# Two float32 filler products of 256 columns between the landings of the last expert's left columns

## The chip, the cores and the metric

The kernel runs on one core of one Trainium2 chip. The metric is the device time of one execution in microseconds; lower is better. TensorE (PE) multiplies, VectorE (DVE) and ScalarE (ACT) evict from PSUM and do elementwise work, GpSimd (POOL) issues the loads that change the type, and SyncE (SP) issues the stores.

## The reference: pooled attention, then a mixture of experts by slots

```python
# q, k, v: (8, 8, 576, 64); k and v are means over 8 positions: 72 keys
scores = scale * q @ k_p.T;  attn = softmax(scores);  x = attn @ v_p
# x as (4608, 512); phi: (512, 32); w1: (8, 512, 1024); w2: (8, 1024, 512)
logits = x @ phi
d = softmax(logits, over tokens);  slot_input = d.T @ x     # 32 slots, 4 per expert
for e in range(8):
    slot_out[e] = relu(slot_input[e] @ w1[e]) @ w2[e]
c = softmax(logits, over slots);  out = c @ slot_out        # (4608, 512)
```

Inputs and output are float32; the kernel computes in bfloat16 with float32 sums.

## The kernel before

**The first part** goes over four pairs of batches. For each it pools keys and values, turns the queries, computes scores and attention, and collects the slots' inputs. The exponentials of all tokens' logits, transposed, stay in the tile cT. POOL's queue issues all weight loads, which change float32 to bfloat16 on the way: w1 to its own tile, w2 of experts 0 to 3 into `big`, of 4 and 5 into `qTa`, of expert 6 into `xsa` in two loads (chunks 0 to 4, chunks 5 to 7; lines 482 and 483). w2 of the last expert, 7, comes in six loads of its own (line 499): first the left 256 columns in the three PIECES of chunks 0 to 2, 3 to 6 and 7, then the right 256 columns in the same three.

**The second part** starts at line 511. There the order of PE, ACT, DVE and SP is that of the text: each engine runs its instructions in the order in which they are written, and waits where a semaphore makes it wait. `hidden` and `turn_hidden` compute the first layer for all experts. `second_layer(e, j0, j1, half)` adds chunks j0 to j1 of expert e to `so_ps`, one product a chunk; with `half` only the left or right 256 columns. Four chunks in a row go to four strips of 32 columns of the array, and so run beside each other.

`busy(n)` (line 583) multiplies a 128 by 128 float32 view of cT with n columns of the same view, into the scratch tile `idle`, which nothing reads. The kernel before calls it five times, with 512 columns each time: around the row sums (lines 665 to 668), after expert 5 (line 671) and in the middle of expert 6 (line 673).

**The place of the change** is lines 674 to 677: the second half of expert 6, then chunks 0 to 2 of the last expert's left columns, which wait for the first landing, then chunks 3 to 6, which wait for the second, then `begin(0)`. In `begin` ScalarE scales the sum so far into `so_a` (line 625). TensorE multiplies the carried part of chunk 7 (`from_z`, line 630) and `so_a` (line 633) for the first four tiles of the output; then it adds chunk 7 to `so_ps`, and ScalarE makes the final `so` (line 648). `tiles` and the loop at line 685 make the other tiles: one product each (line 611), an eviction by ACT (line 588) or DVE (line 590) that divides by the row sum, and stores by SP (line 607): eight of 256 KB for the first eight tiles, in halves, then 1, 1, 2 and 3 MB.

Of the kernel before, what the change touches and what calls it, by code (L numbers as in the profile page):

```python
# [18 lines left out]
def kernel(  # L19
# [525 lines left out]
    def second_layer(e, j0=0, j1=FJ, half=None):  # L545
        cols = slice(0, DM) if half is None else halves[half]
        for fj in range(j0, j1):
            g = fj % NG
            nc.tensor.matmul(out=so_ps[g * NS:(g + 1) * NS, cols], lhsT=hT[:, e, fj],
                             rhs=w2_at[e, fj] if half is None else w2_half[fj, half],  # L550
                             start=(e == 0 and fj < NG), stop=(e == E - 1 and fj >= NG), skip_group_check=True)
# [31 lines left out]
    def busy(n):  # L583
        nc.tensor.matmul(out=idle[:, 0:n], lhsT=cTf[:, 0:128], rhs=cTf[:, 0:n], start=True, stop=True)
# [37 lines left out]
    def begin(half):  # L622

        cols = halves[half]
        scaled(0, so_a[:, cols], so_ps[:, cols], recC)
        f = [ps_f.tile([128, DM], FP, name="f_ps", tag="f")[:, 0:HC] for _ in range(CARRY)]

        def from_z(n, j0, j1):
            for j in range(j0, j1):
                nc.tensor.matmul(out=f[n], lhsT=zT[:, j - J7, n], rhs=w2_half[j, half], start=(j == J7), stop=False)  # L630

        def from_slots(n):
            nc.tensor.matmul(out=f[n], lhsT=tokens(n), rhs=so_a[:, cols], start=False, stop=True)  # L633

        for n in range(2):
            from_z(n, J7, FJ - 1)
        for n in range(2):
            from_z(n, FJ - 1, FJ)
        for n in range(2):
            from_slots(n)  # L640
        put(0, cols, 0, f[0])
        put(1, cols, 1, f[1])
        store(0, 0, 2, cols)
        second_layer(E - 1, J7, FJ, half)
        for n in range(2, CARRY):
            from_z(n, J7, FJ)
            from_slots(n)
        scaled(0, so[:, cols], so_ps[:, cols], recC)
        put(2, cols, 1, f[2])
        put(3, cols, 0, f[3])  # L650
        store(0, 2, 4, cols)
# [20 lines left out]
    second_layer(E - 2, 0, 5)  # L672
    busy(512)
    second_layer(E - 2, 5, FJ)
    second_layer(E - 1, 0, 3, 0)
    second_layer(E - 1, 3, J7, 0)
    begin(0)
    tiles(4, 6, 0)
# [41 lines left out]
```

## Time and profile before

| | us |
|---|---|
| median of 3 runs | 175.56 (175.49 to 175.78) |
| the profiled execution's own time | 175.54 |
| its span, first to last instruction | 173.8 |
| PE busy | 128.0 (74%) |
| DVE busy | 93.0 (54%) |
| ACT busy | 89.1 (51%) |
| POOL busy | 21.7 (12%) |

The profile is of one execution. The span runs from the first to the last instruction; the time of the execution has what lies around it as well. The page cuts the span into 40 slices of 4.3 us and gives the busy share of each engine in tenths. Other views list groups of instructions by line, the chain of work that ended last, the instructions in order of time, and the busy time, granted TensorE clock and DMA share in stretches that one can choose. In a row of the timeline stand the start, the busy time, the engine, the line and the tiles, and in brackets the idle time before it with what ended it. Matmuls are pipelined and their ends are modelled; a few records can be missing. A DMA share above 1 means that transfers overlapped on an engine.

### The profile page before, as it was taken

How to read it: one execution, taken by the hardware profiler on the slowest of the kernel's cores; microseconds unless marked ns; L12 is line 12 of the kernel's file. 1: busy time of each engine (PE TensorE's matmuls, PEld its weight loads, DVE VectorE, ACT ScalarE, POOL GpSimd, SP SyncE). 2: the span in 40 equal slices, each digit the busy share in tenths (PEclk: the TensorE clock that was granted, in tenths of full speed). 3: DMA queues.
4: the chain of work that ended last, by engine and by line, in shares of the span. 5: the costliest groups of instructions: out<-in, count | busy, mean ns of one | idle time of the engine just before them, and what ended most of it. 6: DMA issues, size and time to landing. Idle time of an engine off the chain costs nothing.

```text
span 173.8 us, 2847 instructions
## 1 busy us (share of the span) xinstructions
PE 128.0 (74%) x1104; PEld 69.0 (40%) x1104; DVE 93.0 (54%) x255; ACT 89.1 (51%) x171; POOL 21.7 (12%) x37
## 2 busy tenths in 40 slices
PE   0005787999899999999699999637999995897000
PEld 0002443665555665556444665422453322432000
DVE  5403344397868589786972856750542002799000
ACT  3201249885887739888490895463021103898000
POOL 7000111022100040009000104001410000000000
PEclk9999999999999999999957999955799999999555
DMA  5999999999999999999999999999999999999994
GB/s 192 247 216 223 216 216 212 220 214 212 218 218 214 215 219 214 218 215 214 215 219 211 223 211 219 213 221 211 223 211 219 208 197 177 301 390 447 404 453 183
DMA packets 8989, 41.13 MB, mean 237 GB/s; under 512 B 640, under 2 KB 4736, under 8 KB 5136
## 3 DMA queue, kind: packets, MB, share of 16 engines
q0 software_dynamic: 6080, 30.48, 85.5%
q1 hardware_dynamic: 2896, 10.49, 15.3%
q8 instruction: 8, 0.13, 0.3%
q14 instruction: 5, 0.04, 0.1%
HBM read 61.93 MB, written 9.44 MB: 411 GB/s over the span
## 4 chain that ended last, share of the span: by engine, by line
PE 40%; DMA 20%; ACT 16%; DVE 11%; issue 4%; POOL 1%; DVEq 0%; ACTq 0%; POOLq 0%
DMA xsa<-in_moe_w_dram 14%; PE pool_ps L227 9%; ACT exa L301 7%; DMA phi_f<-in_moe_phi_dram 7%; PE u_ps L314 6%; PE sc L299 6%; PE G_ps L349 4%; PE q_ps L259 4%; DVE w_sb L590 4%; DVE xsa L325 4%; PE lg_ps L342 2%; PE turn_ps L243 2%; ACT vmeans L233 2%; DVE rec L319 2%; PE f_ps L611 2%
## 5 line engine op out<-in xcount | busy, mean ns | idle before, releaser
L301 ACT ACTIVATE exa<-sc 72x576 bf16<-72x576 f32 x64 | 39.3, 653 | 6.6 <-PE u_ps L314 3.4
L325 DVE TENSOR_TENSOR xsa<-u_ps,rec 128x384 bf16<-128x384 f32 x66 | 35.8, 553 | 1.2
L314 PE MATMUL u_ps<-vp,exa 72*128 72x97 bf16 (+1 forms) x304 | 25.0, 215 | 4.6 <-DVE xsa L325 3.6
L314 PEld LDWEIGHTS <-exa 72*128 72x128 bf16 (+1 forms) x320 | 17.7, 103 | 15.6 <-DVE xsa L325 6.1
L299 PE MATMUL sc<-qTa,kp 64*72 64x288 bf16 x128 | 22.0, 313 | 1.6 <-ACT exa L301 1.0
L227 PE MATMUL pool_ps<-big,pmat 128*128 128x512 bf16 x64 | 17.5, 398 | 0.7 <-ACT qTa L263 0.6
L319 DVE RECIPROCAL rec<-u_ps 128x4 f32<-128x4 f32 x69 | 11.2, 174 | 11.5 <-PE u_ps L314 11.2
L179 PE MATMUL phi_ps<-spread,sel 128*128 128x256 bf16 x4 | 1.3, 394 | 15.1 <-DVE spread L174 15.1
L349 PE MATMUL G_ps<-xsa,ee 128*128 128x512 bf16 x36 | 11.5, 481 | 1.2 <-ACT ee L343 1.2
L259 PE MATMUL q_ps<-ident,big 128*128 128x128 bf16 x144 | 11.6, 219 | 0.8 <-DVE qTa L265 0.2
L299 PEld LDWEIGHTS <-kp 64*72 64x72 bf16 x128 | 7.9, 109 | 8.4 <-issue 3.0
L235 DVE TENSOR_REDUCE rsum<-rest_ps 128x64 f32<-128x512 f32 x8 | 5.5, 692 | 9.6 <-PE rest_ps L231 9.6
L265 DVE COPY qTa<-q_ps 128x768 bf16<-128x768 bf16 x16 | 8.7, 552 | 3.1 <-PE q_ps L259 3.0
L611 PE MATMUL f_ps<-so,cT 128*128 128x512 bf16 (+1 forms) x36 | 9.6, 353 | 0.7 <-ACT w_sb L588 0.6
L259 PEld LDWEIGHTS <-big 128*128 128x128 bf16 x144 | 8.6, 97 | 3.3 <-issue 1.8
L590 DVE TENSOR_SCALAR w_sb<-f_ps,recR 128x512 f32<-128x512 f32 x14 | 9.3, 741 | 0.1
L263 ACT COPY qTa<-q_ps 128x768 bf16<-128x768 bf16 x8 | 6.4, 795 | 5.7 <-PE q_ps L259 5.7
L590 DVE TENSOR_SCALAR exa<-f_ps,recR 128x256 f32<-128x256 f32 x8 | 3.8, 483 | 9.9 <-PE f_ps L633 9.6
L233 ACT CAST vmeans<-pool_ps 128x1024 bf16<-128x1024 f32 x4 | 4.0, 1012 | 9.2 <-PE pool_ps L227 9.2
L227 PEld LDWEIGHTS <-pmat 128*128 128x128 bf16 x64 | 5.9, 101 | 6.8 <-issue 2.1
L588 ACT ACTIVATE w_sb<-f_ps,recR 128x512 f32<-128x512 f32 x14 | 8.4, 696 | 0.2
L499 POOL DMA_DIRECT2D xsa<-in_moe_w_dram x6 | 4.1, 695 | 27.4 <-PE G_ps L349 13.2
(109 smaller groups left out, 160.9 us busy)
## 6 DMA issues: line engine op xcount, KB each, us to landing
w_sb<-in_moe_w_dram POOLq DMA_DIRECT2D x2, 3072.0 KB, 38.3
big<-in_q_dram POOLq DMA_DIRECT2D x4, 1152.0 KB, 12.8
big<-in_v_dram POOLq DMA_DIRECT2D x4, 1152.0 KB, 16.7
big<-in_moe_w_dram POOLq DMA_DIRECT2D x1, 4096.0 KB, 32.3
big<-in_k_dram POOLq DMA_DIRECT2D x3, 1152.0 KB, 21.4
out_dram<-w_sb SPq DMA_DIRECT2D x1, 3072.0 KB, 10.9
w_sb<-in_moe_w_dram POOLq DMA_DIRECT2D x2, 1024.0 KB, 19.6
qTa<-in_moe_w_dram POOLq DMA_DIRECT2D x1, 2048.0 KB, 33.2
```

The lines of the kernel that those rows point to most:

```text
L227: nc.tensor.matmul(out=ps, lhsT=pmat, rhs=src[:, t:full * POOL:POOL, :], start=(t == 0), stop=(t == POOL - 1))
L259: nc.tensor.transpose(out=ps[:, t].rearrange("p n i -> p (n i)"), in_=q_sb[pair][:, tt:tt + 2, :].rearrange("p t d -> p (t d)"), identity= ...
L265: nc.vector.tensor_copy(out=dst, in_=ps)
L299: nc.tensor.matmul(out=ps[:, r, 0:S // 2], lhsT=kp[pair][rows, n], rhs=qT[pair][rows, n].rearrange("p t i -> p (t i)"), start=True, stop=True)
L301: nc.scalar.activation(out=dst.rearrange("p r (i t) -> p r i t", t=NU), in_=ps[:, :, 0:S // 2].rearrange("p r (t i) -> p r i t", i=NI), fu ...
L314: nc.tensor.matmul(out=ps[rows, hh], lhsT=ex[b][:, hh].rearrange("p r t -> p (r t)")[:, c:c + rows.stop - rows.start], rhs=vp[(2 * pair + ...
L319: nc.vector.reciprocal(out=rec, in_=ps[:, :, XW])
L325: nc.vector.tensor_tensor(out=dst, in0=ps[:, :, 0:XW], in1=rec.rearrange("p h -> p h ()").to_broadcast([128, HQ, XW]), op=ALU.mult)
L349: nc.tensor.matmul(out=ps, lhsT=ee[:, t].rearrange("p g s -> p (g s)"), rhs=x[:, t, :, 0:D], start=(t == 0), stop=(t == 8))
L588: nc.scalar.activation(out=dst, in_=src, func=AF.Copy, scale=by)
L590: nc.vector.tensor_scalar(out=dst, in0=src, scalar1=by, scalar2=None, op0=ALU.mult)
L611: nc.tensor.matmul(out=ps, lhsT=tokens(n), rhs=so[:, cols], start=True, stop=True)
```

## The change

Two calls of `busy(256)` are added to the written order: one between the last chunks of expert 6 and chunks 0 to 2 of the last expert's left columns, one between these and chunks 3 to 6.

```diff
     second_layer(E - 2, 0, 5)
     busy(512)
     second_layer(E - 2, 5, FJ)
+    busy(256)
     second_layer(E - 1, 0, 3, 0)
+    busy(256)
     second_layer(E - 1, 3, J7, 0)
     begin(0)
     tiles(4, 6, 0)
```

The function that is called is unchanged:

```python
    def busy(n):
        nc.tensor.matmul(out=idle[:, 0:n], lhsT=cTf[:, 0:128], rhs=cTf[:, 0:n], start=True, stop=True)
```

## The prediction

> **What bounds the kernel now.** I read the page's slices first, for what is busy at the end, then the chain of work that ended last, then the TensorE timeline around the place of the change, then the stores.
>
> ```profile
> DMA  5999999999999999999999999999999999999994
> ```
>
> The DMA engines are busy from the second slice to the last but one. TensorE is not: the change sits in a stretch in which it waits for weights.
>
> The chain of work that ended last (start, us, step) passes that stretch:
>
> ```profile
> 121.63 23.80 DMA xsa<-in_moe_w_dram
> 145.47 0.32 PE so_ps L549 x4
> 145.81 0.48 ACT so_a L588
> 146.33 0.28 PE f_ps L633
> 146.64 0.34 ACT exa L588
> 147.01 0.48 ACT so L588
> 147.53 0.38 PE f_ps L611 x2
> 148.13 0.34 PE f_ps L611 x2
> 148.49 0.47 ACT exa L588
> 148.97 0.37 ACT so_a L588
> 149.38 0.28 PE f_ps L633
> 149.69 0.47 ACT exa L588
> ```
>
> For 23.8 us the chain is one transfer, the second piece of the last expert's left columns. From 145.47 it is a relay of TensorE and ScalarE steps. So what counts is whether the four products at 145.47 start when their weights land, and how fast the relay behind them runs. The TensorE rows of the timeline (start, busy us, operation, then idle time before it and what ended it):
>
> ```profile
> 142.04 1.12 PE L584 MATMUL idle_ps<-cT 128*128 128x512 f32 x2
> 143.18 0.40 PE L549 MATMUL so_ps<-xsa,hT 128*32 128x512 bf16 x3
> 144.18 0.29 PE L549 MATMUL so_ps<-xsa,hT 128*32 128x256 bf16 x3 [0.60 <-DMA xsa<-in_moe_w_dram]
> 145.47 0.29 PE L549 MATMUL so_ps<-xsa,hT 128*32 128x256 bf16 x4 [1.00 <-DMA xsa<-in_moe_w_dram]
> 145.81 0.38 PE L630 MATMUL f_ps<-xsa,zT 128*128 128x256 bf16 x2
> ```
>
> Each call of busy(512) is two float32 passes in the trace. The three products of expert 6's last chunks end at 143.58. TensorE then waits 0.60 us for the first left piece, runs three products, waits 1.00 us for the second, runs four, and goes on. The two fillers go into these two waits.
>
> Behind the relay stand the stores, by the DMA issues of the SP queue (first and last start, us):
>
> ```profile
> L607 SPq DMA_DIRECT2D out_dram<-exa x8: 372/422/455, 147.3 to 152.1; - x8
> L607 SPq DMA_DIRECT2D out_dram<-w_sb x4: 332/338/345, 153.3 to 161.2; - x4
> out_dram<-w_sb SPq DMA_DIRECT2D x1, 3072.0 KB, 10.9
> ```
>
> The last store leaves at 161.2 and takes 10.9 us to land. I take it that a shift of the relay shifts the end by as much. That is an upper bound for either sign, since a store that stands in a queue hides part of a shift.
>
> **The change, part by part.** Nothing is removed or moved. Two calls of busy(256) are added, each one float32 product of a cT block with 256 columns of cT into the scratch tile idle_ps, which no one reads. By the x2 of the row above that is two weight loads and two matmuls a call, so four of each in all. There are no new DMAs, no new waits on another engine (cT was written long before) and nothing for SP, POOL, ScalarE or VectorE. What can be late is what stands behind a filler on TensorE: the three products on the first piece, the four on the second, and through them ScalarE's so_a.
>
> The trace has no float32 product of 256 columns. These rows bound it:
>
> ```profile
> L584 PE MATMUL idle_ps<-cT x10: 590/592/697, 136.2 to 142.6; 128*128 128x512 f32 x10
> L611 PE MATMUL f_ps<-so,cT 128*128 128x512 bf16 x28 | 8.3, 377 | 0.6 <-ACT w_sb L588 0.6
> ...
> L611 PE MATMUL f_ps<-so,cT 128*128 128x256 bf16 x8 | 1.4, 272 | 0.1
> 143.09 0.19 PEld L549 LDWEIGHTS <-hT 128*32 128x32 bf16 x4 [0.76 <-issue]
> 141.73 0.38 PE L549 MATMUL so_ps<-xsa,hT 128*32 128x512 bf16 x1
> ```
>
> Step by step:
>
> - From 512 to 256 columns a bf16 product falls by 377 - 272 = 105 ns. A float32 pass of 512 columns takes 592 ns, that is 215 ns above bf16, so it streams like 1024 bf16 columns and its half saves 2 x 105 = 210 ns.
> - busy(512) holds the engine from 142.04 to 143.09, where the next product's weight load starts: 1.05 us. For 256 columns I estimate 1.05 - 2 x 0.21 = 0.63 us. The ends of the range are nothing (all of it beside other work) and the 1.05 us of the wide form (no saving at all). I take 0.63, because the bf16 pair shows that time goes with columns.
> - The last product ahead of a filler started at 141.73 and the filler at 142.04: 0.31 us. So the first new filler starts at 143.18 + 0.31 = 143.49 and is through at 144.12. With the 0.09 us from the weight load at 143.09 to the product at 143.18, the products on the first piece could start at 144.21. They start at 144.18 now: 0.03 us late, and nobody waits for them before the second piece.
> - The second filler starts at 144.21 + 0.31 = 144.52, is through at 145.15, and the four products could start at 145.24. Their weights let them start at 145.47. So 0.23 us are left, and both fillers are covered by the landings. Price: nothing.
> - If that cover were gone, the price would be what sticks out. With 1.05 us each, the first is through at 144.54 (products at 144.63), the second runs 144.94 to 145.99, and the four products start at 146.08: 0.61 us late.
>
> Below nothing the added work could come out only through TensorE's clock in the relay. By windows (stretch, length, PE busy, ..., granted clock, DMA share, GB/s):
>
> ```profile
> 82.98:86.39 3.41, 2.15 (x28) 1.17 (x26) 3.19 (x10) 0.88 (x3) 0.00 (x0) 1.00 1.04 219
> 86.39:89.81 3.42, 3.36 (x23) 1.61 (x24) 2.74 (x9) 3.17 (x6) 0.00 (x0) 0.50 1.03 216
> 110.29:113.70 3.41, 1.95 (x24) 1.28 (x24) 2.41 (x10) 1.29 (x6) 0.00 (x0) 1.00 1.03 216
> 113.70:117.11 3.41, 0.99 (x8) 0.64 (x8) 2.10 (x7) 2.37 (x11) 0.00 (x0) 0.50 1.03 216
> 141.01:144.42 3.41, 2.80 (x15) 0.70 (x14) 0.00 (x0) 0.00 (x0) 0.00 (x0) 1.00 1.31 192
> 144.42:147.83 3.41, 2.15 (x18) 1.08 (x14) 0.97 (x2) 1.64 (x4) 0.00 (x0) 1.00 1.23 166
> 147.83:151.25 3.42, 2.98 (x24) 1.61 (x24) 2.30 (x5) 2.97 (x8) 0.00 (x0) 1.00 0.91 301
> 143.20:146.60 3.40, 1.61 (x14) 0.67 (x13) 0.00 (x0) 0.47 (x1) 0.00 (x0) 1.00 1.45 195
> ```
>
> The clock is 1.00 throughout 141.01 to 151.25, so in this execution there is nothing for a filler to win. But it fell to 0.50 at 86.39 and at 113.70, after 3.41 us with TensorE busy 2.15 and 1.95 us. These two times lie 27.31 us apart, eight times 3.41, and so do the edges that I chose here. The stretch 144.42 to 147.83, with the same 2.15 us, kept its clock. A stretch of the same length that began at 143.20 has only 1.61 us. Had the edges lain there, the clock would by these rows have been halved in the middle of the relay.
>
> The Trainium skill speaks against a win here: "TensorE: Matmul & The Clock Gate", section on HAM oscillation, gives as its rule no idle gaps above about 3.4 us. With a longest gap of 1.00 us here the clock is never at stake by that rule, and the fillers are worth nothing. The trace doesn't bear the rule out as a bound: ahead of 86.39 the longest idle time in the timeline is well under a microsecond.
>
> ```profile
> 85.09 0.36 PE L314 MATMUL u_ps<-vp,exa 72*128 72x97 bf16 x4 [0.50 <-DVE xsa L325]
> ```
>
> The same page (Part 1) says that the window of about 3.4 us runs freely and isn't tied to the kernel's start; the distance of eight times 3.41 agrees, and one trace can't show where the edges lie in other executions.
>
> Sum: nothing on the path. The profiled execution took 175.54 us, 1.74 more than its span of 173.8, and the median of the runs shown is 175.56, 0.02 above it. **Forecast: 175.5 us, no change.** A measurement of this kernel can tell about 0.2%, or 0.35 us, from no change.
>
> **The rivals.**
>
> *The clock (faster).* If the edges of those 3.41 us stretches lie differently in most executions, the clock is half from about 146.6 to 150.0 before the change, and the fillers prevent it: they bring that stretch from 1.61 us to 1.61 + 2 x 0.63 = 2.87 us busy. The price of half clock, from the same nine products at full and at half clock:
>
> ```profile
> 105.23 2.10 PE G_ps L349 x9
> 119.61 4.02 PE L349 MATMUL G_ps<-xsa,ee 128*128 128x512 bf16 x9 [1.22 <-ACT ee L343]
> ```
>
> That is (4.02 - 2.10) / 9 = 0.21 us for 512 columns, and 0.11 for 256. The relay has two, two and one such products between 147.53 and 149.66: five, 0.5 us. So this rival gives 175.56 - 0.5 = 175.05 us; with a product more or less on the path, 174.9 to 175.2. For it: the trace halves the clock after stretches busier than the one at 143.20. Against it: the execution that kept its clock took 175.54, and the three runs spread only from 175.49 to 175.78. Were most of them slowed by half a microsecond, the profiled one should lie 0.5 us below them, and it doesn't.
>
> *The filler is too long (slower).* If a float32 pass of 256 columns costs as much as one of 512, the four products start 0.61 us late, as worked out above, and the relay and the stores with them: 176.15 us. It decides from the point at which both fillers together take more than 2 x 0.63 + 0.23 = 1.5 us. Landings closer together than now would do the same. For it: 0.23 us isn't much, and the width of the float32 form is not in the trace. Against it: the bf16 rows go with columns.
>
> *No effect at all, because nothing runs in the gap.* Were the fillers' result thrown away by the compiler, the time would be the same 175.5; the existing fillers, also never read, appear in the trace, so I give it no chance of its own.
>
> **How the numbers follow.** Hidden fillers, unchanged clock: 0.58, with its own range 175.3 to 175.8 from the spread of the three runs and 0.2 us of luck below. The clock: 0.28. The filler too long: 0.14. These are also the chances of within 0.2%, faster and slower. The range goes from 175.0 to 176.0: it takes in most of the clock's 174.9 to 175.2 and the half of the slower case in which the fillers stick out by less than 0.45 us.
>
> **What would show it.** Right: four more passes of L584 (x14 instead of x10) with some 380 ns each, the idle times of 0.60 and 1.00 us almost gone, the four products still starting within 0.1 us of 145.47 with a DMA as their releaser, the relay as it was. The clock rival: the relay from 146.6 to 150 shorter than now in the changed kernel, or a kernel before that shows 0.50 there in another execution. The slower rival: the four products released by no DMA, and later than 145.6. The forecast is wrong if the landings themselves move, or if a shift of the relay of some tenths, in either direction, shows in the time.

## The result, and the profile after

The changed kernel is slower: a median of 176.81 us (175.55 to 177.88, 22 runs) against 175.92 us (175.49 to 177.25, 22 runs) for the kernel before, measured side by side. The ratio is 1.0037 with a 95% interval of 1.0019 to 1.0055. The forecast was 175.5 us and no change. In the tables and ranges below, three executions far outside all others (230.06, 209.3 and 198.64 us) and one slow run of the changed kernel (178.66 us, over 1.5% above its fastest) are left out.

The lowest runs of the two kernels are the same, 175.55 and 175.49 us. The profiled execution of the changed kernel took 176.39 us (span 174.6), 0.85 more than that of before. Its fillers are what was forecast. The group of the scratch tile in the profile after:

```profile
L584 PE MATMUL idle_ps<-cT x14: 379/593/697, 137.6 to 146.0; 128*128 128x512 f32 x10, 128*128 128x256 f32 x4
```

Four passes more, 379 ns where the prediction had some 380. The surprise is in the TensorE timeline of the profile after (start, busy us, operation, idle time before it):

```profile
126.61 3.64 PE L528 MATMUL h_ps<-w_sb,siT 128*32 128x512 bf16 x64
...
144.50 0.40 PE L549 MATMUL so_ps<-xsa,hT 128*32 128x512 bf16 x3
144.82 0.70 PE L584 MATMUL idle_ps<-cT 128*128 128x256 f32 x2
145.45 0.29 PE L549 MATMUL so_ps<-xsa,hT 128*32 128x256 bf16 x3
145.67 0.70 PE L584 MATMUL idle_ps<-cT 128*128 128x256 f32 x2
146.30 0.29 PE L549 MATMUL so_ps<-xsa,hT 128*32 128x256 bf16 x4
146.52 0.39 PE L630 MATMUL f_ps<-xsa,zT 128*128 128x256 bf16 x2
```

A filler holds TensorE from 144.82 to 145.45, 0.63 us as estimated. But no bracket with a DMA is left: TensorE waits for no landing. It reaches expert 6's last products at 144.50, not 143.18, so the weights of the first piece already lie there, and both fillers stand in its way. The chain of waits says the same. Where the chain of before had 23.8 us of one transfer, that of after runs through TensorE:

```profile
143.51 1.06 PE idle_ps L584 x2
144.57 0.33 PE so_ps L549 x3
144.89 0.63 PE idle_ps L584 x2
145.74 0.63 PE idle_ps L584 x2
146.37 0.25 PE so_ps L549 x4
```

The trace's record of the second piece's landing is 145.43 us before and 145.68 after. The four products start at 145.47 and at 146.30. So of the 0.83 us, 0.25 are the landing, and 0.58 are the fillers, which stick out behind it. The later landing isn't their doing: expert 6's first chunks landed at 141.55 instead of 141.23, also late, over 3 us ahead of the first filler. The same second landing was at 145.72 in `e7` below, which has no filler there, and at 145.46 in `e15`, the changed kernel again. The relay that follows isn't slower: the end comes 29.73 us after the first product of `from_z` before (175.54 - 145.81) and 29.87 us after (176.39 - 146.52).

TensorE is late from further up. The first layer started at 125.21 in the profile before; here are that row, and then two rows of the profile after:

```profile
125.21 3.64 PE L528 MATMUL h_ps<-w_sb,siT 128*32 128x512 bf16 x64
```

```profile
105.92 2.12 PE L349 MATMUL G_ps<-xsa,ee 128*128 128x512 bf16 x9
...
121.06 3.98 PE L349 MATMUL G_ps<-xsa,ee 128*128 128x512 bf16 x9 [1.22 <-ACT ee L343]
```

Against 105.23 and 119.61 in the rows of before, that is 0.69 us late at the third pair's gather and 1.45 at the last. Of the 0.69 us, 0.54 were there at the start of the kernel: the first product of line 231 starts at 18.80 us before and at 19.34 after, and the seven of line 227 ahead of it take 2.50 us before and 2.87 after. That looks like half clock, but isn't shown: the windows read 1.00 there in both. For the 0.76 us that came in between the two gathers the clock gives the reason. By windows, after:

```profile
107.79:111.20 3.41, 2.84 (x48) 2.09 (x45) 2.82 (x9) 1.37 (x4) 0.58 (x2) 1.00 1.03 216
111.20:114.62 3.42, 2.71 (x23) 1.87 (x20) 1.96 (x7) 1.28 (x6) 0.00 (x0) 0.50 1.05 220
114.62:118.03 3.41, 1.20 (x11) 0.65 (x8) 1.78 (x7) 1.84 (x9) 0.00 (x0) 0.50 1.02 214
118.03:121.44 3.41, 1.52 (x5) 0.56 (x6) 0.57 (x2) 2.15 (x5) 0.00 (x0) 0.50 1.03 216
121.44:124.86 3.42, 3.42 (x9) 1.22 (x8) 0.00 (x0) 0.00 (x0) 2.53 (x4) 0.50 1.06 223
```

Four stretches of 3.41 us at half clock, from 111.20, where the profile before had three, from 113.70. Between the products that start at 111.04 and at 114.31 in the profile before, which mostly run while only the execution after is at half clock, its lateness grows from 0.75 to 1.44 us. The fillers of the change, which run 20 us behind these stretches, can't have caused this, and `e15` below, the same kernel, has three such stretches, from 114.05. It is how that execution fell.

### The profile page after: what moved, and what is told of

It reads as the page before. It is cut to its first block, busy times and chain, and to the rows that moved or that the text cites. A ratio compares the mean times of both kernels' runs of the same rounds, so it can differ in the third digit from the quotient of the medians.

```text
span 174.6 us, 2855 instructions
## 1 busy us (share of the span) xinstructions
PE 130.3 (75%) x1108; PEld 70.2 (40%) x1108; DVE 92.9 (53%) x255; ACT 89.0 (51%) x171; POOL 21.7 (12%) x37
## 4 chain that ended last, share of the span: by engine, by line
PE 54%; ACT 15%; DVE 12%; DMA 7%; issue 4%; POOL 1%; DVEq 0%; ACTq 0%; POOLq 0%
PE pool_ps L227 9%; ACT exa L301 7%; PE u_ps L314 7%; DMA phi_f<-in_moe_phi_dram 7%; PE G_ps L349 6%; PE sc L299 6%; PE q_ps L259 4%; DVE w_sb L590 4%; PE idle_ps L584 4%; DVE xsa L325 3%; PE so_ps L549 3%; PE lg_ps L342 2%; PE R_ps L418 2%; PE h_ps L528 2%; PE turn_ps L243 2%
## 5 line engine op out<-in xcount | busy, mean ns | idle before, releaser
L314 PE MATMUL u_ps<-vp,exa 72*128 72x97 bf16 (+1 forms) x304 | 25.7, 218 | 4.1 <-DVE xsa L325 3.9
L314 PEld LDWEIGHTS <-exa 72*128 72x128 bf16 (+1 forms) x320 | 18.2, 104 | 15.4 <-DVE xsa L325 6.5
## 6 DMA issues: line engine op xcount, KB each, us to landing
big<-in_q_dram POOLq DMA_DIRECT2D x4, 1152.0 KB, 12.8
```

What stands on the lines that cost most here:

```text
L314: nc.tensor.matmul(out=ps[rows, hh], lhsT=ex[b][:, hh].rearrange("p r t -> p (r t)")[:, c:c + rows.stop - rows.start], rhs=vp[(2 * pair + ...
```

## The experiments

Three theories were set against each other. **Arrival**: TensorE comes to the landings earlier or later, by how long its clock was half ahead of them; the waits there absorb some of that, and the fillers use this room up. **Contention**: the fillers slow the landings or the relay themselves, in every execution. **Luck**: the fillers do nothing, and the changed kernel only drew worse executions. Each result lists the mean granted clock of each execution; one stretch more at half clock lowers it by 3.41 x 0.5 / 174 = 0.0098. The mean counts half clock behind the relay too, so it is a rough sign of a late TensorE, not a measure.

**Both kernels again.** `e0_before_again` is the kernel before, `e15_after_again` the changed kernel, both without an edit.

> The kernel before, unchanged, for the time of each execution beside its mean granted clock. Theory 'arrival': TensorE comes to the landings earlier or later, as the clock was half for three, four or more stretches of 3.41 us ahead of them (a mean clock of about 0.916, 0.907, 0.898); the waits of 0.60 and 1.00 us absorb the first loss. So: at 0.915 and above 175.5 to 175.6, at 0.907 175.7 to 176.2 (the changed kernel has 176.1 to 177.1 there), at 0.898 176.5 to 177.0 (the changed kernel 177.0 to 177.9). Rival 'luck': the fillers do nothing, the changed kernel only drew more executions of lower clock; then the times at each mean clock are those of the changed kernel. Rival 'contention': the fillers slow the landings or the relay in every execution; then the changed kernel would be slower at 0.916 too, against 175.55 to 175.62 measured.

> The changed kernel, unchanged, on the same chip as the other three: 176.0 to 176.9 in the median; below 175.65 where the mean clock is 0.915 or above, 176.1 to 177.1 at 0.906 to 0.909, above 177 at 0.90 and below, if the state of the clock ahead of the landings sets what the fillers cost.

Measured: the kernel before 176.15 us against itself at 175.65 (ratio 1.0014, 0.9987 to 1.0040), which shows how much a median of 12 wanders; the changed kernel 176.78 us against 175.60 (1.0048, 1.0010 to 1.0085). All runs of both whose clock is listed, by mean clock:

| mean clock | changed: runs, median (range) | before: runs, median (range) |
|---|---|---|
| 0.914 and above | 9, 175.57 (175.52 to 175.63) | 33, 175.55 (175.44 to 176.44) |
| 0.904 to 0.910 | 14, 176.74 (176.09 to 177.07) | 50, 175.57 (175.44 to 176.59) |
| below 0.904 | 10, 177.46 (176.96 to 178.11) | 58, 175.81 (175.55 to 177.92) |

(14 more of before lie between 0.910 and 0.914.) At a high clock the fillers cost nothing, so contention in every execution falls. One stretch of half clock more, and the changed kernel loses 1.2 us where the kernel before mostly loses none, so luck falls; nor did the changed kernel draw a worse clock (27% of its runs at 0.914 and above, 21% of those of before). Below 175.85 us are 27% of the changed kernel's runs and 72% of those of before. The expectation for `e0` had the kernel before paying more than it does: 175.7 to 176.2 us in the middle row and 176.5 to 177.0 in the last, where 175.57 and 175.81 were measured. That for `e15` held but for one run of 176.96 us in the last row, where above 177 was expected.

The profiled execution of `e15_after_again` happened to be an early one, 175.57 us. Its TensorE timeline:

```profile
125.44 3.64 PE L528 MATMUL h_ps<-w_sb,siT 128*32 128x512 bf16 x64
...
143.31 0.40 PE L549 MATMUL so_ps<-xsa,hT 128*32 128x512 bf16 x3
143.64 0.70 PE L584 MATMUL idle_ps<-cT 128*128 128x256 f32 x2
144.27 0.29 PE L549 MATMUL so_ps<-xsa,hT 128*32 128x256 bf16 x3
144.49 0.70 PE L584 MATMUL idle_ps<-cT 128*128 128x256 f32 x2
145.50 0.29 PE L549 MATMUL so_ps<-xsa,hT 128*32 128x256 bf16 x4 [0.31 <-DMA xsa<-in_moe_w_dram]
```

This is the forecast to a few hundredths: both fillers in the waits, and the four products released by the DMA with 0.31 us to spare. The same kernel gives 175.57 or 176.39 us as the first layer starts at 125.44 or at 126.61. The other profiles agree on the clock: of the 14 without added work ahead of the gather that can be used, the five with three stretches at half clock in a row there (before, `e0`, `e10`, `e15`, `e17`) have the first layer at 125.21 to 125.44 us, and the nine with four at 126.56 to 128.30. From the third pair's gather to the last, the five take 14.37 to 14.40 us and the nine 15.06 to 15.14: so the fourth stretch goes with some 0.75 us. The rest of the lateness, up to 2.3 us (`e7`: third gather at 107.57 instead of 105.23), lies ahead of the third gather, and about half of it or more is there within the first 25 us.

**One filler at a time, and both ahead of the landings.**

```diff
# e1_first_only
-    busy(256)            # the second
# e2_second_only
-    busy(256)            # the first
# e3_ahead: both ahead of expert 6's last chunks
+    busy(256)
+    busy(256)
     second_layer(E - 2, 5, FJ)
-    busy(256)
     second_layer(E - 1, 0, 3, 0)
-    busy(256)
     second_layer(E - 1, 3, J7, 0)
```

> Only the first filler, between expert 6 and chunks 0 to 2. Arrival: 0.63 us of the 1.6 us of waits are used up, so a late execution (mean clock 0.907) loses up to 0.3 us and one at 0.898 up to 0.63; median about 0.2 to 0.3 us above the kernel before, about half of what both cost. Contention or luck: no relation to the number of fillers under luck (ratio 1.000); half the cost under contention, but at 0.916 as well.

> Only the second filler, between chunks 0 to 2 and 3 to 6. Arrival: the same as with the first filler alone, since what counts is TensorE's time ahead of the four products on the second landing, or a little more, because after the first landing only 1.0 us of wait is left to hide it: 0.2 to 0.4 us above before in the median. If the place mattered (contention with the transfer that is on the chain), clearly more than the first alone.

> Both fillers moved ahead of expert 6's last chunks, so that none stands between the landings; the same 1.26 us of TensorE time lies ahead of the four products. Arrival: the same cost as the changed kernel, ratio 1.003 to 1.005, and 175.5 to 175.7 at a mean clock of 0.916 (with the products on the first landing late but not those on the second). If the place between the landings is what costs (contention with these transfers, or the wake-up after a wait), the ratio is near 1.000.

Measured, against 175.65 us: 176.34 (ratio 1.0021, 0.9989 to 1.0052), 175.86 (1.0001, 0.9973 to 1.0029) and 176.49 us (1.0026, 0.9995 to 1.0058). The intervals all reach 1, so these medians decide nothing, and what was expected of them is neither confirmed nor refuted. The profiles tell more. That of `e2_second_only` had its first layer at 128.1:

```profile
145.98 0.50 PE L549 MATMUL so_ps<-xsa,hT 128*32 128x512 bf16 x6
146.41 0.70 PE L584 MATMUL idle_ps<-cT 128*128 128x256 f32 x2
147.04 0.29 PE L549 MATMUL so_ps<-xsa,hT 128*32 128x256 bf16 x4
```

and that of `e3_ahead`, at 127.5, with the fillers within the x6 and none between the landings:

```profile
144.32 1.99 PE L584 MATMUL idle_ps<-cT 128*128 128x512 f32 x6
146.24 0.61 PE L549 MATMUL so_ps<-xsa,hT 128*32 128x512 bf16 x10
```

There the four products start at 146.48, 1.1 us behind their landing at 145.33, and the execution took 176.65 us. So fillers that stand between no landings cost too, if they stand on TensorE ahead of the four products. But their place sets how much. From the start of the first layer to that of the four products, in profiles in which no wait for a landing is left:

| fillers of 256 columns | us |
|---|---|
| none (`e13`, described below) | 18.10 |
| one between the groups (`e1`, `e2`) | 18.84, 18.94 |
| both ahead, behind `busy(512)` (`e3`) | 18.97 |
| both between the groups (after, `e16`) | 19.69, 19.69 |

Between the groups the two fillers add 1.6 us, more than their 1.26; together behind another filler they add 0.9.

**The size of the fillers.** `e4_bf16` has bfloat16 products of 256 columns in the same places, `e5_wide` the float32 ones with 512.

```diff
# e4_bf16: lhsT=cT[:, 0, 0:128], rhs=cT[:, 0, 0:n]
-    busy(256)
+    busy16(256)
# e5_wide
-    busy(256)
+    busy(512)
```

> The fillers in the same two places, but in bfloat16 with 256 columns: one pass of some 0.1 us of TensorE time instead of 0.63. Arrival: 0.2 us in all, a ratio of 1.000 to 1.001. If the mere presence of an instruction between the landings costs, the ratio stays at about 1.004.

> Both fillers with 512 columns, 1.05 us each instead of 0.63. Arrival: in a late execution (mean clock 0.907 or 0.898) 0.84 us more than the changed kernel, 177.3 to 178.7, and now also a cost on time (0.916): about 0.6 us, 176.1. Median ratio to before about 1.008 to 1.010. Luck: no change against 1.000 to 1.004. Contention: twice the cost in every execution.

Measured: 176.35 us (1.0034, 1.0008 to 1.0059) and 177.25 us (1.0086, 1.0061 to 1.0110). The wide ones have the expected ratio, with a range of only 177.18 to 177.40. But all these runs have a mean clock of 0.914 or 0.915, where 176.1 was expected. The profile is late all the same (first layer at 126.56, four stretches at half clock ahead of it); the half clock at its end began at 165.77 us instead of 162.40 in the profile after, which is where the higher mean comes from. The bfloat16 ones miss the expectation: they should have cost next to nothing, and have nearly the 1.004 that was expected if the mere presence of an instruction there costs. The TensorE timeline of `e4_bf16`:

```profile
144.97 0.40 PE L549 MATMUL so_ps<-xsa,hT 128*32 128x512 bf16 x3
145.30 0.28 PE L584 MATMUL idle_ps<-cT 128*128 128x256 bf16 x1
145.51 0.29 PE L549 MATMUL so_ps<-xsa,hT 128*32 128x256 bf16 x3
145.74 0.28 PE L584 MATMUL idle_ps<-cT 128*128 128x256 bf16 x1
145.95 0.29 PE L549 MATMUL so_ps<-xsa,hT 128*32 128x256 bf16 x4
```

From products to products are 0.54 and 0.44 us, where without a filler the three start 0.01 us after the three before them (144.97 is the start of expert 6's last ones; in `e2_second_only` the two groups are the one x6 at 145.98). So here a product over the whole array between groups that share it by strips cost more than its own 0.1 us: from the first layer to the four products are 18.86 us, 0.76 more than without fillers. With its first layer at 127.1, this execution was late enough to pay: the four products came 0.46 us behind the landing at 145.49, and it took 176.0 us. That explains this execution; why 11 of 12 runs lie above 175.85 isn't settled by it.

**Less TensorE time ahead of the landings.** `e6` takes the filler behind expert 5 (line 671) from the changed kernel, `e10` from the kernel before; `e7` takes those of lines 671 and 673 from the kernel before; `e11` and `e14` (the same kernel twice) take them from the changed kernel.

```diff
     for e in range(4, E - 2):
         second_layer(e)
-    busy(512)                 # e6, e7, e10, e11, e14
     second_layer(E - 2, 0, 5)
-    busy(512)                 # e7, e11, e14
     second_layer(E - 2, 5, FJ)
```

> The changed kernel without the filler of 512 columns behind expert 5: 1.05 us less TensorE time ahead of the landings, against the 1.26 us added. Arrival: within 0.2% of the kernel before (ratio 0.999 to 1.001). Contention between the fillers and the landings: as the changed kernel, 1.004. If the filler taken away kept the clock up, 0.50 shows in the relay from 144 on and the time is above 177.

> The kernel before without the two fillers of 512 columns behind expert 5 and within expert 6: TensorE arrives 2.1 us earlier. Arrival: late executions are absorbed too, the median falls to about 175.6, ratio 0.997 to 0.999, and the spread shrinks - if the clock holds. If it doesn't, some executions have half the clock in the relay and lose 0.5 us and more, and the median stays at 176 or rises.

> The kernel before without the 512-column filler behind expert 5 alone: TensorE arrives 1.05 us earlier. Arrival: an execution is free up to a first layer at 128.1 us instead of 127.1, so nearly all are at 175.5 to 175.8; ratio 0.998 to 0.999, as long as the clock in the relay holds. If it falls, 0.5 us more in those executions, and the median is 176.0 to 176.1.

> The two 256-column fillers between the landings instead of the two 512-column ones behind expert 5 and within expert 6: 2.10 us taken away, 1.26 us added, so TensorE is 0.84 us less late than in the kernel before. Arrival: median 175.6 to 175.8. The clock in the relay decides the rest: with the fillers between the landings it should hold more often than without any (where it fell to 0.50 at 147.4 in the profile and the median was 176.47); if it falls, 176.0 and above.

> The kernel with the two 256-column fillers in place of the two of 512, once more, as its first interval was 0.994 to 1.001 with one stray run: 175.5 to 175.6 in the median and 9 in 10 runs below 175.85; ratio to before 0.997 to 0.999.

| kernel | median (range), us | ratio to before |
|---|---|---|
| e6, changed less 671 | 175.78 (175.53 to 176.48) | 1.0006 (0.9990 to 1.0021) |
| e7, before less 671 and 673 | 176.47 (176.14 to 178.38) | 1.0047 (1.0016 to 1.0079) |
| e10, before less 671 | 175.57 (175.48 to 177.18) | 0.9999 (0.9964 to 1.0035) |
| e11, changed less 671 and 673 | 175.56 (175.41 to 176.96) | 0.9978 (0.9942 to 1.0013) |
| e14, the same again | 175.58 (175.50 to 176.91) | 0.9994 (0.9970 to 1.0018) |

`e6` gives most of the loss back by taking TensorE time away: from the first layer to the four products its profile has 18.52 us, 1.17 less than the changed kernel's 19.69. `e7` shows what a filler can be worth: without any there, TensorE waits again, and no run is below 176.14. The windows of its profile:

```profile
143.99:147.40 3.41, 1.77 (x19) 0.90 (x15) 0.35 (x1) 0.94 (x3) 0.00 (x0) 1.00 1.36 184
147.40:150.81 3.41, 3.35 (x20) 1.18 (x17) 1.58 (x4) 2.30 (x7) 0.00 (x0) 0.50 0.75 225
```

After a stretch with 1.77 us busy the clock is half in the relay. The longest wait ahead of it is 1.06 us:

```profile
145.76 0.29 PE L549 MATMUL so_ps<-xsa,hT 128*32 128x256 bf16 x4 [1.06 <-DMA xsa<-in_moe_w_dram]
```

By the rule of the Trainium skill weighed in the prediction ("TensorE: Matmul & The Clock Gate", HAM oscillation: no gaps above about 3.4 us) the clock should have held; the trace differs, and decides.

The end comes 30.35 us after the first product of `from_z` (176.51 - 146.16) instead of some 29.8: 0.55 us, where the prediction's clock rival had 0.5. With the two narrow fillers put back (`e11`, `e14`), 20 of 23 runs are below 175.85. That is the largest share of all kernels here (`e10`: 9 of 12), but their intervals don't separate them from the kernel before, and `e14` missed its expected ratio of 0.997 to 0.999. That the clock holds in the relay is seen in the profile of `e14` alone.

**Bringing TensorE early on purpose.** Fillers into a spare PSUM bank, between the last pair's products and ahead of the gather (lines 490 to 493), should keep the clock up from 110 to 121 us. `e8` and `e9` have 19 in bfloat16, in the kernel before and in the changed one; `e12` and `e13` six in float32, in the changed one and in the kernel before; `e16` four of these six, in the changed one.

```diff
     for i in range(5):
         u_tile(*last[:2], 4 + i, ...)
+        keep(...)       # e8, e9: 3 of 512; e12, e13: 1 of 256; e16: the same, for i >= 2
     weigh(x, ee, 0, 9)
+    keep(...)           # e8, e9: 4 of 512; e12, e13, e16: 1 of 512
     gather(x, G_ps, ee, 0, 9)
```

> The kernel before with 19 bfloat16 fillers of 512 columns in the waits of the last pair's products, ahead of the gather (110 to 121 us), to keep the clock up there. Theory 'arrival': the half clock there (10 to 14 us of it in each execution so far) is what makes TensorE late; with a full clock the first layer starts at about 123 us instead of 125.2 to 128.3, all waits on landings are back, and the late executions vanish: median 175.5 to 175.7, no run above 176 - unless the longer waits now lower the clock in the relay, which costs 0.5 us (0.50 shows at 144 to 151). Rival 'arrival comes from elsewhere' (the order of the work in the first part): the first layer still starts anywhere from 125 to 128 and the median stays at 175.6 to 176.2.

> The same 19 fillers in the changed kernel. Arrival: TensorE comes early, both new fillers of 0.63 us fall into waits and cost nothing: median 175.5 to 175.7, equal to the warm kernel before within 0.1%, and 1.2 us below the changed kernel's late executions. If the fillers between the landings cost by themselves, it stays 0.4% above the warm kernel before.

> The changed kernel with six float32 fillers (five of 256 columns, one of 512; six instructions of the program instead of 19) ahead of the gather. The 19 brought TensorE early, but an instruction load of 16 KB then fell on one DMA engine at 157.7 and its share of the stores ended 1.8 us late; with six the load should not come within the stores. Arrival: where the first layer starts before 125.8 us, both fillers between the landings fall into waits: median 175.5 to 175.8 and most runs below 175.85, against 176.5 to 176.8 for the changed kernel of the same call. If the fillers between the landings cost by themselves, it stays with the changed kernel.

> The same six float32 fillers in the kernel before. Arrival: TensorE early, 175.5 where the clock holds in the relay; with longer waits on the landings and no fillers in them, 0.50 there in a part of the executions (as at 147.6 with the 19) and then 176.0 to 177: median 175.5 to 176.1, at or above the changed kernel with the same six.

> The changed kernel with four instead of six float32 fillers ahead of the gather, so that TensorE's program is five rows longer than that of the kernel before, as in the kernel whose stores met no instruction load (seven rows longer did). Arrival: first layer at 125.8 us or earlier in most executions, both fillers between the landings in waits, median 175.5 to 175.9 with two runs in three below 175.85, against 175.6 for the kernel before and 176.8 for the changed kernel on the same kind of chip. If the fillers between the landings cost by themselves: 176.4 and above. If the load comes all the same: 177.3 and above.

| kernel | median (range), us | ratio to before | first layer, us |
|---|---|---|---|
| e8, before, 19 | 177.39 (177.25 to 179.42) | 1.0101 (1.0043 to 1.0159) | 124.32 |
| e9, changed, 19 | 177.57 (177.05 to 178.41) | 1.0096 (1.0067 to 1.0126) | 124.83 |
| e12, changed, 6 | 178.16 (177.40 to 178.48) | 1.0113 (1.0075 to 1.0151) | 125.58 |
| e13, before, 6 | 175.70 (175.46 to 177.15) | 0.9993 (0.9965 to 1.0021) | 128.19 |
| e16, changed, 4 | 176.14 (175.55 to 177.76) | 1.0032 (1.0003 to 1.0061) | 127.99 |

`e8` and `e12` have 6 runs each. In time, none of the changed ones came to the expected 175.5 to 175.9. In the profiles of `e9` and `e12` TensorE is early and the fillers are covered, as this row of `e12_warm32_after` shows, against 146.30 in the profile after. `e12` started much like that profile (the product of line 231 at 19.23 us, 19.34 after), so its first layer at 125.58 instead of 126.61 shows that the fillers ahead of the gather bring 1.0 us:

```profile
145.51 0.29 PE L554 MATMUL so_ps<-xsa,hT 128*32 128x256 bf16 x4 [0.17 <-DMA xsa<-in_moe_w_dram]
```

The relay and the issue of the last store (161.26 us, against 161.22 before) are then those of before. What is late is that store's landing. From the DMA views of `e12_warm32_after`, from 154 to 163 us:

```profile
q8 instruction: 1, 0.02, 0.7%
...
out_dram<-w_sb SPq DMA_DIRECT2D x1, 3072.0 KB, 12.8
```

One transfer of instructions, 16 KB, runs at 160.17 among the stores, and the last store takes 12.8 us instead of 10.9. From 171.0 to 172.2 the DMA share is 0.05, about one engine of the 16, where the kernel before has 0.01: so one engine seems to have fallen behind, though the trace doesn't name it. `e8` and `e9` have such a transfer too, at 159.76 and 157.67, and last stores of 12.5 and 12.7 us; all other profiles but that of `e11` have 10.9 to 11.0 and no such transfer there. `e8` has half clock in the relay besides, from 147.56 to 154.39, where no filler stands between the landings. `e13` and `e16` have no such transfer, but the profiled executions were late all the same (first layer at 128.19 and 127.99), so that `e16` doesn't test what it was made for: the early arrival didn't come. These two were late from the start: the product of line 231 starts at 20.14 and 20.01 us instead of 18.80 and takes 0.63 us instead of 0.38, and some 2.3 us of lateness are there before 26 us. So the fillers ahead of the gather, which act some 90 us later, couldn't have prevented it. That `e13` came out far below `e12`, where no less was expected, goes with the transfer in `e12`.

**Is it the length of the program?** `e17` adds four products of 16 columns at the very start of the kernel before.

```diff
+        for _ in range(4):
+            nc.tensor.matmul(out=x_ps[:, 0:16], lhsT=ident, rhs=ident[:, 0:16], start=True, stop=True)
         phi_ps = ps_m.tile([128, H, NS], FP, name="phi_ps", tag="m")
```

> The kernel before with four products of 16 columns at the very start, where TensorE waits for its first data: eight rows more in its program and no work anywhere near the landings. If the length of the program alone brings the instruction load of 16 KB into the stores (from seven rows more): one 16 KB instruction transfer at about 160 us, one DMA engine 1.8 us behind the others, and 177.3 in the undisturbed executions, 1.010 times before. If it hangs on the fillers ahead of the gather: 175.5 to 175.6.

Measured: 175.70 us (1.0006, 0.9994 to 1.0019), and no such transfer. The expectation counted rows of the program, in which a float32 product is one row but four instructions of the profile. By the profiles' instructions, `e17` has 2855, like the changed kernel, and those with the transfer among the stores have 2879 (`e12`), 2882 (`e8`) and 2890 (`e9`), those without up to 2871 (`e13`). A length between 2871 and 2879 would fit all of them, but `e17` was too short to test it.

**One law for the profiles.** In the 15 profiled executions with a full clock in the relay and no instruction transfer among the stores (`e11` has none that can be used), the time is the start of the first `from_z` product plus 29.69 to 29.87 us. That start follows the four products, and these start at the later of two times: some 0.04 us after the second landing, or where TensorE's own work ends. This work takes 16.29 us from the first layer to expert 6's first products, then 1.60, and in the changed kernel 0.95 and 0.85 us: 19.69 in all. So, with the landing of the profile before, the changed kernel loses nothing up to a first layer at 145.47 - 19.69 = 125.78 us. Without fillers the last two steps are some 0.2 us together, and the kernel before is free up to 145.47 - 18.10, about 127.4. The profiled executions of the kernels without added work ahead of the gather have their first layers at 125.21 to 128.30.

## Why the prediction was wrong

- **The cost of a filler** was right: 0.63 us estimated and measured, 379 ns a pass. The steps from group to group were taken as 1.03 us each and measured as 0.95 and 0.85, so this term erred on the safe side.
- **What bounds the kernel** was right for the profiled execution, and only for it. The chain through the second landing is one state of the kernel; in the changed kernel's profile the chain is TensorE's.
- **"So 0.23 us are left, and both fillers are covered by the landings"** is the step that failed. It took TensorE's arrival from one execution (143.18) as if it were fixed. In `e15_after_again`, with nearly that arrival, 0.31 us were left. In the profile after, with an arrival at 144.50, 0.58 us stuck out. The room that the change used up, 1.6 us of the some 2.2 between a first layer at 125.21 and one at 127.4, was not idle: it is what absorbs a late execution.
- **The clock rival** had the right price (0.5 us, measured 0.55 in `e7`), but the wrong place. The text saw that the edges of the 3.41 us stretches can lie differently in other executions, and asked only what this does to the relay. It didn't ask what it does to the half clock at 113.70, ahead of the change, where one stretch more goes with a late TensorE. That the changed kernel's relay ran at full clock in both its profiles agrees with the kernel before, so the fillers won nothing there.
- **The slower rival** named a filler that is too long. The fillers were of the expected length; the waits were shorter. Its test, four products released by no DMA and later than 145.6, is what the profile shows, for another reason.
- **The three runs from 175.49 to 175.78** were taken as the spread. With 22 runs of the same kernel it was 175.49 to 177.25. The tail was the sign that the waits are sometimes used up, and three runs didn't show it.

The room, what fills it and what sticks out are shown. That half clock further up goes with a late TensorE is seen in the profiles and in the table by mean clock, but it gives only a part of the lateness (after, 0.76 of 1.45 us at the last gather); making it early on purpose gave the expected start of the four products, but not a clean time, because of the instruction transfer. What decides in an execution where the edges fall, and how late TensorE is from the kernel's start on, stays open.

## What to carry to other kernels

A wait in front of a landing is room for lateness, and one profile shows only how much was left that time: before putting work into it, look at how the arrival varies over executions, by the spread of many runs and their mean clock. A filler that keeps the clock up is worth having where TensorE is early and is paid for in full where it is late, so a kernel that already has fillers gains more likely by moving them than by adding some; here that gave the most runs below 175.85 us, but no difference clear of the noise. And the price of a filler is what it adds to the way to the next landing, not its own length: between groups that run beside each other it was higher.

## What the runs showed of the hardware that was not expected

- A bfloat16 filler of 256 columns between groups of products that share the array by strips set the groups 0.44 and 0.54 us apart, where two groups without one started 0.01 us apart. The two added 0.76 us to the way to the four products, several times their own 0.1 us of columns each.
- In the three profiles with an instruction transfer of 16 KB among the stores, at 157.7 to 160.2 us, the last store took 12.5 to 12.8 us instead of 10.9 to 11.0, though the transfer itself ran for only 0.92 to 0.95 us. A DMA share of 0.05 near the end suggests that one of the 16 engines was behind; that the transfer is the cause is inferred.
- Half clock began after stretches of 3.41 us with TensorE busy 1.77 us (`e7`), 1.95 and 2.15 us (before) and 2.84 us (after, at 111.20), and did not after another with 2.15 us. The busy time of the profile alone doesn't tell when the clock falls.
